# Attention with beacon tokens into a max-out FFN: quads' second halves by another queue, and a new opening order

## The chip, the cores and the metric

The kernel runs on one NeuronCore of a Trainium2 chip. The core has five instruction streams, each of which runs its own list in order: TensorE (PE, matrix products and transposes through it), VectorE (DVE), ScalarE (ACT), GpSimd (POOL) and SyncE (SP, which here only starts transfers). Transfers between the memory of the chip (HBM) and the core's on-chip memory are issued by SP, ACT or POOL, each to a queue of its own, and are carried out by 16 DMA engines. The metric is the time of one execution on the device in microseconds; of several executions the median is given.

## The reference

Eight batches of eight heads, 576 tokens of 64 features, and 16 "beacon" keys and values per head that every token may see. Causal attention over beacons and tokens is followed by an FFN that takes the maximum of three products:

```python
k_all = np.concatenate([beacon_k, k], axis=2)
v_all = np.concatenate([beacon_v, v], axis=2)
scores = scale * np.matmul(q, k_all.transpose(0, 1, 3, 2))
scores = np.where(causal, -1000000000.0, scores)
a = np.exp(scores - scores.max(-1, keepdims=True))
a /= a.sum(-1, keepdims=True) + 1e-09
attn = np.matmul(a, v_all)                      # (B, H, S, D)
x = attn.transpose(0, 2, 1, 3).reshape(4608, 512)
h = np.maximum(np.maximum(x @ w1, x @ w2), x @ w3)   # 512 -> 768
out = h @ w_out                                      # 768 -> 512
```

Inputs and output are FP32.

## The kernel before

All matrix work is done in BF16. Heads go in pairs (pair p is heads 2p and 2p+1 of its batch, with four pairs to a batch), and two pairs make a quad, that is half a batch. The order of every instruction is written out by hand: `first_steps` (line 901) is the opening and `loop_steps` (line 1075) is the rest. `emit_all` walks the lists, and each entry appends its instructions to the streams of the engines that it uses. An entry that stands early therefore also stands early on each of its engines, and an instruction that waits holds back everything behind it on that engine.

What the entries of the opening do:

- `load half p i` (`load_half`, line 221) brings the first 288 tokens of q (i = 0) or k (i = 1) of one pair as FP32 over the named queue, and `cast half` makes BF16 of it.
- `load quad half g h` (`load_quad`, line 237) brings half h of q and of k for the four heads of quad g of batch 0. It is issued by POOL, whose queue turns FP32 into BF16 on the way.
- `half p h bank q_copy idle idle_q` (`turn_half`, line 428) transposes q and k of one pair on PE (line 440) and copies the results into qT and kT (line 448): k by DVE, q by the named engine. `idle_q` and `idle` are numbers of pairs of filler transposes ahead of q's and of k's (`fill`, line 404).
- `load keys`, `cast keys`, `turn keys` bring the beacon keys, and `keys p` places a batch's beacon keys ahead of pair p's in kT.
- `scores p gi idle` (`emit_scores`, line 503) runs `idle` filler matmuls (`spare`, line 476), multiplies kT and qT for group gi of pair p (line 514) into one of two PSUM buffers, and ACT writes the exponential to `at_sb` (line 523). For batch 0, group 0 holds all that the first 288 tokens need.
- `mask p gi` (`emit_masks`, line 529) puts zeros above the diagonal, by DVE (line 540) or POOL (line 542).
- `load v0 t` and `cast v0 t` bring v of batch 0 in five tiles and cast them (line 328). A load with an engine's name is gated: that engine first writes one element of the destination, so the transfer is issued only when that engine has come so far in its list.
- `values quad hf` (`emit_pv`, line 561) sums the exponentials and multiplies them with v (line 583). `invert` (lines 604 and 606, ACT) and `multiply` (line 616, DVE) divide by the sums and write xT.
- `load w i` (`load_w`, line 335) brings one of the three FFN weights, as two transfers issued by POOL. `ffn bank kind` (`mm1_halves`, line 634) is one step of the FFN's first layer on 256 tokens: two column blocks, each over all four parts of the features, so it needs both transfers of its weight. DVE then copies the result (line 630) or takes the maximum with it (line 632).
- `load quad` and `whole` do for a quad of batch 1 what the halves do for batch 0; `load v`, `load pair` and `load` bring later batches by SP, in FP32, into eight staging buffers (`new_stage`, line 192) that are cast on chip.
- `busy n cols` is filler before any data has come.

After the opening four PSUM buffers are in use, and scores, FFN steps and the second layer alternate on PE to the end.

Of the kernel before, what the change touches and what calls it, by code (L numbers as in the profile page):

```python
# [9 lines left out]
BF16 = mybir.dt.bfloat16  # L10
# [6 lines left out]
def kernel(  # L17
# [15 lines left out]
    B, H, S, D = q.shape  # L33
# [12 lines left out]
    QP = S // QR  # L46
    HR = QR // 2
# [11 lines left out]
    PPQ = PPB // n_quad  # L59
# [41 lines left out]
    def head(g, j):  # L101
        return 4 * g + j
# [12 lines left out]
    early = early_stack.enter_context(tc.tile_pool(name="early", bufs=1))  # L115
# [42 lines left out]
    ring = [(sc_psum, "sc"), (sc_psum, "sc")]  # L158
# [30 lines left out]
    stage = {}  # L189
    v_tiles = {}  # L190

    def new_stage(key):
        stage[key] = st_pool.tile([128, STW], FP32, name="st")
        return stage[key]
# [21 lines left out]
    def half_source(g, h, i, j0, n):  # L216
        hs = slice(head(g, j0), head(g, j0) + n)
        src = (q, k)[i][0, hs, HALF * h : HALF * (h + 1)]
        return src.rearrange("h (p r) d -> p h (r d)", r=HR)

    def load_half(p, i, queue):
        st = half_pool.tile([QP, 2, HR, D], FP32, name=f"h32{i}")
        queue.dma_start(
            out=st.rearrange("p h r d -> p h (r d)"),
            in_=half_source(p // PPQ, 0, i, 2 * (p % PPQ), 2),
        )
        stage["half", p, i] = st
# [6 lines left out]
        )  # L234
        stage["half16", p, 0, i] = t16

    def load_quad(g, h):
        for i in range(2):
            t16 = early.tile([QP, 4, HR, D], BF16, name=f"quad{g}{h}{i}")
            nc.gpsimd.dma_start(  # L240
                out=t16.rearrange("p h r d -> p h (r d)"), in_=half_source(g, h, i, 0, 4)
            )
            for j in range(PPQ):
                stage["half16", PPQ * g + j, h, i] = t16[:, 2 * j : 2 * j + 2]

    def load_whole_quad(b, g):
        for i, src in enumerate((q, k)):
            t16 = early.tile([QP, 4, QR, D], BF16, name=f"whole{b}{g}{i}")
            nc.gpsimd.dma_start(
                out=t16.rearrange("p h r d -> p h (r d)"),  # L250
                in_=src[b, head(g, 0) : head(g, 4)].rearrange("h (p r) d -> p h (r d)", r=QR),
            )
            for j in range(PPQ):
                stage["whole", b * PPB + PPQ * g + j, i] = t16[:, 2 * j : 2 * j + 2]
# [94 lines left out]
    def load_beacons(b0, b1, dst, queue=None):  # L349
        for b in range(b0, b1):  # L350
            (queue or nc.sync).dma_start(
                out=dst[Nb * (b - b0) : Nb * (b - b0 + 1)],
                in_=beacon_k[b].rearrange("h n d -> n h d"),
            )
# [485 lines left out]
    def start_late():  # L840
# [9 lines left out]
    by = {"dve": by_dve, "act": by_act, "pool": by_pool}  # L850
    queue = {"sp": nc.sync, "act": nc.scalar, "q pool": nc.gpsimd}
    idle = {"dve": nc.vector, "pool": nc.gpsimd}
# [3 lines left out]
        "identity": lambda: make_identity(nc, ident),  # L856
        "triangle": make_tri,
        "load half": lambda p, i, e: load_half(p, i, queue[e]),
        "load quad half": load_quad,
        "load keys 0": lambda e: load_beacons(0, 1, bk32_0, queue[e]),  # L860
        "load keys 1": lambda: load_beacons(1, B_PE, bk32_1),
        "load v0": load_first_v,
# [36 lines left out]
        "cast keys 2": lambda e: by[e](bk16, bk32),  # L899
    }  # L900
    first_steps = [
        ("load half", 0, 0, "sp"),
        ("busy", 27, 200),
        ("identity",),
        ("busy", 16, 160),
        ("triangle",),
        ("load quad half", 1, 0),
        ("load half", 1, 0, "act"),
        ("load half", 0, 1, "act"),
        ("cast half", 0, 1, "dve"),  # L910
        ("load keys 0", "act"),
        ("cast keys 0", "act"),
        ("load half", 1, 1, "sp"),
        ("cast half", 0, 0, "act"),
        ("turn keys 0",),
        ("cast half", 1, 0, "pool"),
        ("load v0", 0, "pool"),
        ("cast half", 1, 1, "dve"),
        ("load v0", 1, "pool"),
        ("half", 0, 0, "ffn", "act", 0, 8),  # L920
        ("keys", 1, "act"),
        ("load v0", 2),
        ("half", 1, 0, "pv", "act", 3, 5),
        ("keys", 3, "pool"),
        ("load quad half", 0, 1),
        ("scores", 0, 0, 0),
        ("scores", 1, 0, 0),
        ("load w", 0),
        ("half", 3, 0, "ffn", "dve", 0, 0),
        ("half", 2, 0, "pv", "dve", 4, 0),  # L930
        ("mask", 1, 0, "dve"),
        ("cast v0", 0, "pool"),
        ("cast v0", 1, "act"),
        ("scores", 3, 0, 0),
        ("mask", 0, 0, "dve"),
        ("load v0", 3, "dve"),
        ("keys", 2, "pool"),
        ("cast v0", 2, "act"),
        ("scores", 2, 0, 7),
        ("values", 0, 0, "pv", 0, 4, 0),  # L940
        ("half", 0, 1, "ffn", "act", 0, 9),
        ("invert",),
        ("mask", 3, 0, "dve"),
        ("multiply",),
        ("scores", 0, 2, 4),
        ("mask", 2, 0, "pool"),
        ("load keys 1",),
        ("scores", 0, 3, 0),
        ("values", 1, 0, "ffn", 0, 4, 0),
        ("load quad half", 1, 1),  # L950
        ("invert",),
        ("multiply",),
        ("mask", 0, 2, "pool"),
        ("scores", 0, 1, 0),
        ("half", 1, 1, "pv", "act", 1, 0),
        ("load v0", 4, "dve"),
        ("scores", 1, 2, 4),
        ("mask", 0, 1, "pool"),
        ("cast v0", 3, "act"),
        ("ffn", "ring", 0),  # L960
        ("ffn", "ffn", 0),
        ("mask", 1, 2, "dve"),
        ("scores", 1, 3, 0),
        ("scores", 1, 1, 0),
        ("half", 2, 1, "pv", "dve", 0, 0),
        ("mask", 1, 3, "dve"),
        ("ffn", "ffn", 0),
        ("half", 3, 1, "pv", "dve", 0, 0),
        ("load v", 1, 0, "dve"),
        ("cast v0", 4, "dve"),  # L970
        ("mask", 0, 3, "dve"),
        ("mask", 1, 1, "dve"),
        ("scores", 2, 3, 0),
        ("scores", 2, 2, 7),
        ("load w", 1),
        ("scores", 3, 2, 0),
        ("mask", 2, 3, "dve"),
        ("cast keys 1", "dve"),
        ("values", 0, 1, "pv", 0, 4, 0),
        ("turn keys 1",),  # L980
        ("invert",),
        ("scores", 3, 3, 0),
        ("ffn", "ffn", 0),
        ("load quad", 1, 0),
        ("load w", 2),
        ("mask", 3, 3, "dve"),
        ("multiply",),
        ("load pair", 9, "pool"),
        ("scores", 2, 1, 0),
        ("mask", 2, 2, "pool"),  # L990
        ("ffn", "ffn", 0),
        ("mask", 2, 1, "pool"),
        ("scores", 3, 1, 0),
        ("keys", 6, "dve"),
        ("keys", 4, "pool"),
        ("ffn", "ring", 0),
        ("mask", 3, 1, "dve"),
        ("keys", 5, "dve"),
        ("mask", 3, 2, "pool"),
        ("whole", 4, "ffn", "dve"),  # L1000
        ("values", 1, 1, "pv+", 0, 4, 0),
        ("invert",),
        ("scores", 4, 1, 0),
        ("multiply",),
# [722 lines left out]
```

## Time and profile before

| what | value |
|---|---|
| median of 3 runs | 285.77 us (285.26 to 286.31) |
| the profiled execution | 285.21 us, span 283.3 us |
| PE busy | 276.3 us, 98% of the span |
| DVE, ACT, POOL busy | 176.5, 154.5, 143.4 us |
| the first scores on PE | at 8.75 us |
| the first FFN step on PE | at 19.47 us |

The span is the part of the execution in which the program's instructions run; the time contains some two microseconds around it. A row of the timeline or of the chain begins with the start and the length of a piece of work in us, then the engine, the name of what it writes and the line. A row of the waits names who waited for whom, for how long in total, how often, and the longest. A row of the groups ends with busy time, the mean in ns, and the idle time ahead of the group. A row on transfers gives their number, the size of one and the us from issue to landing. A row of the windows has the stretch, its length, each engine's busy time with its number of instructions, the granted share of PE's clock, and the busy time of the DMA engines as a share, which is over 1 where several queues are served at once.

### The profile page before, as it was taken

Reading aid. Unit: us, or ns where it says so; the run is one execution under the profiler, and the core shown is the slowest. Engines: PE = TensorE matmul, PEld = TensorE weight load, DVE = VectorE, ACT = ScalarE, POOL = GpSimd, SP = SyncE. Lnnn points to the kernel's source line nnn. Section 1 sums busy time; section 2 is a strip of 40 time slices with the busy share of each in tenths; the row PEclk is TensorE's granted clock in tenths of the full one; section 3 lists DMA queues with packets and bytes.
Section 4 is the critical chain, followed back from the end, with each engine's and each line's share of the span. In section 5 each row is a group of like instructions: output and inputs, shape, how many; then the busy total and the mean of one; then the engine's idle time right before and its main releaser. Section 6 shows DMA issues by size and latency. Waiting matters only on the chain.

```text
span 283.3 us, 11781 instructions
## 1 busy us (share of the span) xinstructions
PE 276.3 (98%) x5099; PEld 201.5 (71%) x5099; DVE 176.5 (62%) x331; ACT 154.5 (55%) x249; POOL 143.4 (51%) x316
## 2 busy tenths in 40 slices
PE   8999999999999999999999999999999999999995
PEld 7666777757777576768677686767877687757762
DVE  2456777886676765756566666646575665661754
ACT  2876676897563574637464574725765474624000
POOL 4462318898741583758734497508854682400000
PEclk9999999999999999999999999999999999999999
DMA  9999999999978399999999969989999962003004
GB/s 153 168 171 206 223 234 157 247 206 309 211 141 168 45 252 178 171 197 147 189 178 215 236 91 176 166 204 185 217 160 170 163 177 76 2 3 150 2 2 185
DMA packets 118307, 46.27 MB, mean 163 GB/s; under 512 B 107248, under 2 KB 112880, under 8 KB 118256
## 3 DMA queue, kind: packets, MB, share of 16 engines
q1 hardware_dynamic: 111888, 39.20, 75.6%
q0 software_dynamic: 5808, 6.00, 13.0%
q8 instruction: 40, 0.66, 1.1%
q10 hardware_dynamic: 560, 0.33, 0.4%
q14 instruction: 11, 0.09, 0.1%
HBM read 35.13 MB, written 9.44 MB: 157 GB/s over the span
## 4 chain that ended last, share of the span: by engine, by line
PE 91%; DMA 3%; ACT 2%; POOL 1%; DVE 1%; issue 1%; ACTq 0%; POOLq 0%
PE t L700 44%; PE t L726 16%; PE t L583 11%; PE t L514 6%; DMA quad<-in_k_dram 3%; PE pv L478 2%; ACT at_sb L523 2%; PE pv L638 2%; PE sc L514 1%; PE sc L638 1%; PE fps L638 1%; PE t L398 1%; POOL at_sb L542 1%; PE wide L583 1%; PE pv L583 1%
## 5 line engine op out<-in xcount | busy, mean ns | idle before, releaser
L700 PE MATMUL t<-xT,w_sb 64*128 64x288 bf16 (+1 forms) x1008 | 129.6, 285 | 0.0
L700 PE MATMUL t<-xC,wC 64*128 64x288 bf16 (+1 forms) x1008 | 129.6, 285 | 0.0
L523 ACT ACTIVATE at_sb<-t 128x992 bf16<-128x992 f32 (+1 forms) x96 | 82.6, 863 | 42.8 <-PE t L514 37.1
L632 DVE TENSOR_TENSOR hT<-hT,t 128x576 bf16<-128x576 bf16 (+1 forms) x84 | 63.7, 763 | 30.6 <-PE t L700 30.6
L542 POOL TENSOR_SCALAR_AFFINE_SELECT at_sb<-at_sb 128x256 bf16<-128x256 bf16 (+2 forms) x143 | 53.6, 390 | 53.7 <-ACT at_sb L523 41.2
L700 PEld LDWEIGHTS <-w_sb 64*128 64x128 bf16 x1008 | 51.3, 94 | 12.6 <-issue 1.1
L700 PEld LDWEIGHTS <-wC 64*128 64x128 bf16 x1008 | 51.0, 94 | 12.4
L726 PE MATMUL t<-w_out_sb,hT 128*128 128x512 bf16 x210 | 47.9, 380 | 0.0
L681 POOL COPY xC<-xT 64x576 bf16<-64x576 bf16 (+1 forms) x26 | 18.0, 693 | 42.8 <-DVE xT L616 42.5
L630 DVE CAST hT<-t 128x576 bf16<-128x576 f32 (+1 forms) x36 | 27.7, 769 | 14.8 <-PE t L700 14.6
L726 PEld LDWEIGHTS <-hT 128*128 128x128 bf16 x210 | 19.3, 98 | 22.8 <-issue 0.9
L259 POOL CAST p<-st 96x768 bf16<-96x768 f32 x44 | 34.9, 822 | 0.3
L734 DVE COPY y<-t 128x1024 f32<-128x1024 f32 (+1 forms) x20 | 21.8, 1091 | 20.5 <-PE t L726 20.3
L514 PE MATMUL t<-qT,kT 64*128 64x288 bf16 (+4 forms) x288 | 33.1, 279 | 0.0
L616 DVE TENSOR_TENSOR xT<-t,recip 128x288 bf16<-128x288 f32 (+2 forms) x78 | 22.9, 351 | 16.0 <-ACT recip L606 10.7
L604 ACT ACTIVATE lnd<-t 128x288 f32<-128x288 f32 x26 | 10.7, 410 | 36.9 <-PE t L583 36.9
L514 PEld LDWEIGHTS <-kT 64*128 64x128 bf16 x400 | 18.5, 94 | 11.4 <-issue 6.7
L583 PEld LDWEIGHTS <-v_sb 128*32 128x32 bf16 (+1 forms) x1408 | 24.6, 96 | 1.6 <-issue 0.4
L523 ACT ACTIVATE at_sb<-sc 128x736 bf16<-128x736 f32 (+5 forms) x28 | 23.2, 862 | 4.2 <-PE sc L514 4.1
L583 PE MATMUL t<-at_sb,v_sb 128*32 128x96 bf16 (+8 forms) x1144 | 23.3, 228 | 0.0
L316 POOL CAST v_sb<-st 128x1536 bf16<-128x1536 f32 (+2 forms) x21 | 18.4, 894 | 0.6 <-DMA st<-in_v_dram 0.6
L583 PEld LDWEIGHTS <-ones 128*32 128x32 bf16 (+2 forms) x512 | 10.9, 95 | 6.7 <-issue 3.9
(125 smaller groups left out, 220.1 us busy)
## 6 DMA issues: line engine op xcount, KB each, us to landing
out_dram<-y SPq DMA_DIRECT2D x15, 512.0 KB, 4.6
st<-in_q_dram SPq DMA_DIRECT2D x24, 288.0 KB, 5.8
st<-in_k_dram SPq DMA_DIRECT2D x24, 288.0 KB, 6.2
st<-in_v_dram SPq DMA_DIRECT2D x24, 256.0 KB, 5.5
w_sb<-in_moe_w_dram POOLq DMA_DIRECT2D x6, 384.0 KB, 8.9
st<-in_v_dram SPq DMA_DIRECT2D x8, 224.0 KB, 5.1
st<-in_v_dram SPq DMA_DIRECT2D x8, 160.0 KB, 4.7
out_dram<-y SPq DMA_DIRECT2D x5, 256.0 KB, 4.6
```

The costliest lines, as they stand in the source:

```text
L259: cast(t16.rearrange("p r h d -> p h r d"), st[0:QP, i * NQ2 : (i + 1) * NQ2].rearrange("p (h r d) -> p h r d", h=2, r=QR),)
L316: cast(v_sb[0:n, t:t1].rearrange("p t h d -> p (t h d)"), st[0:n, (t - t_lo) * H * D : (t1 - t_lo) * H * D],)
L514: nc.tensor.matmul(ps[:, e, off : off + q1 - q0], kT[hs, 128 * t : 128 * t + 128], qT[hs, q0:q1], start=True, stop=True, tile_position=(64 ...
L523: nc.scalar.activation(out=both_heads(p, gi), in_=ps[:, :, 0 : g_width(p, gi)], func=AF.Exp, scale=scale)
L542: nc.gpsimd.affine_select(out=view, in_=view, compare_op=ALU.is_ge, fill=0.0, base=x0, pattern=[[0, 2], [1, hi - lo]], channel_multiplier=-1,)
L583: nc.tensor.matmul(ps[bank][32 * j : 32 * j + 32, lo + q0 - qa : lo + qb - qa], lhsT, at_view(PPQ * quad + j // 2, t, j % 2, q0, qb), star ...
L616: nc.vector.tensor_mul(xT[:, 2 * g + part - 1, c0 + ca : c0 + cb], ps[bank][:, lo : lo + cb - ca], recip[:, ca:cb],)
L630: (by_i or by_dve)(h, ps)
L632: nc.vector.tensor_max(h, h, ps)
L700: nc.tensor.matmul(ps[:, e], w[own(e), ct, cols], x, start=(ct == 0 and not over), stop=(ct == n_ct - 1 and over), tile_position=(64 * e, 0),)
L726: nc.tensor.matmul(ps[:, u], h_tile(tt + u, ft), w_out_sb[:, ft, :], start=(ft == 0), stop=(ft == n_ft - 1),)
L734: nc.vector.tensor_copy(y[:, 0:n], ps[:, 0:n])
```

## The change

The two second halves of batch 0's quads are issued by SP instead of POOL. They land as FP32, q and k of a quad side by side in one of the eight staging buffers, and a new step casts each of them into the tile in which it landed before. Quad 1's is gated by POOL. The opening's list is put in another order, from the first load to the load of the third weight: other queues carry the first halves, pair 1's scores go first and pair 0's after `half 3 0` and `half 2 0`, the tiles of v come in the order 0, 2, 1, several casts and masks go to other engines, the first weight is loaded behind pair 1's mask, and the numbers of fillers differ. `load pair 9` stands eleven entries further down.

```diff
-    def load_quad(g, h):
+    def load_quad(g, h, queue=None, gate=None):
+        if queue:
+            st = new_stage(("quad", g, h))[0:QP].rearrange("p (i x) -> p i x", i=2)
+            if gate:
+                gate.memset(st[0:1, 0, 0:1], 0.0)
+            for i in range(2):
+                queue.dma_start(
+                    out=st[:, i].rearrange("p (h x) -> p h x", h=4),
+                    in_=half_source(g, h, i, 0, 4),
+                )
+            return
...
+    def cast_quad(g, h, i, cast):
+        st = stage["quad", g, h][0:QP].rearrange("p (i x) -> p i x", i=2)
+        t16 = early.tile([QP, 4, HR, D], BF16, name=f"quad{g}{h}{i}")
+        cast(t16.rearrange("p h r d -> p (h r d)"), st[:, i])
+        for j in range(PPQ):
+            stage["half16", PPQ * g + j, h, i] = t16[:, 2 * j : 2 * j + 2]
+        if ("half16", PPQ * g, h, 1 - i) in stage:
+            stage.pop(("quad", g, h))
...
 first_steps = [
-    ("load half", 0, 0, "sp"),
+    ("load half", 0, 0, "act"),
+    ("load quad half", 1, 0),
     ("busy", 27, 200),
     ("identity",),
     ("busy", 16, 160),
-    ("triangle",),
-    ("load quad half", 1, 0),
-    ("load half", 1, 0, "act"),
     ("load half", 0, 1, "act"),
-    ("cast half", 0, 1, "dve"),
+    ("load half", 1, 1, "act"),
     ("load keys 0", "act"),
+    ("cast half", 0, 0, "dve"),
+    ("load half", 1, 0, "sp"),
+    ("cast half", 0, 1, "act"),
     ("cast keys 0", "act"),
-    ("load half", 1, 1, "sp"),
-    ("cast half", 0, 0, "act"),
+    ("load v0", 0, "dve"),
+    ("half", 0, 0, "pv", "dve", 6, 0),
     ("turn keys 0",),
     ("cast half", 1, 0, "pool"),
-    ("load v0", 0, "pool"),
     ("cast half", 1, 1, "dve"),
+    ("load v0", 2, "pool"),
     ("load v0", 1, "pool"),
-    ("half", 0, 0, "ffn", "act", 0, 8),
+    ("keys", 3, "pool"),
+    ("half", 1, 0, "pv", "act", 0, 0),
     ("keys", 1, "act"),
-    ("load v0", 2),
-    ("half", 1, 0, "pv", "act", 3, 5),
-    ("keys", 3, "pool"),
-    ("load quad half", 0, 1),
-    ("scores", 0, 0, 0),
-    ("scores", 1, 0, 0),
+    ("triangle",),
+    ("scores", 1, 0, 4),
+    ("keys", 2, "pool"),
+    ("cast v0", 0, "dve"),
+    ("mask", 1, 0, "pool"),
+    ("load quad half", 0, 1, "sp"),
+    ("load v0", 3, "dve"),
     ("load w", 0),
     ("half", 3, 0, "ffn", "dve", 0, 0),
-    ("half", 2, 0, "pv", "dve", 4, 0),
-    ("mask", 1, 0, "dve"),
-    ("cast v0", 0, "pool"),
     ("cast v0", 1, "act"),
+    ("half", 2, 0, "pv", "dve", 6, 8),
+    ("scores", 0, 0, 0),
+    ("mask", 0, 0, "dve"),
     ("scores", 3, 0, 0),
-    ("mask", 0, 0, "dve"),
-    ("load v0", 3, "dve"),
-    ("keys", 2, "pool"),
+    ("cast quad half", 0, 1, 0, "dve"),
     ("cast v0", 2, "act"),
-    ("scores", 2, 0, 7),
+    ("scores", 2, 0, 0),
     ("values", 0, 0, "pv", 0, 4, 0),
-    ("half", 0, 1, "ffn", "act", 0, 9),
-    ("invert",),
-    ("mask", 3, 0, "dve"),
+    ("mask", 2, 0, "dve"),
+    ("cast quad half", 0, 1, 1, "pool"),
+    ("load keys 1",),
+    ("half", 0, 1, "ffn", "act", 8, 0),
+    ("invert",),
     ("multiply",),
-    ("scores", 0, 2, 4),
-    ("mask", 2, 0, "pool"),
-    ("load keys 1",),
+    ("scores", 0, 2, 3),
+    ("mask", 3, 0, "pool"),
+    ("load quad half", 1, 1, "sp", "pool"),
     ("scores", 0, 3, 0),
     ("values", 1, 0, "ffn", 0, 4, 0),
-    ("load quad half", 1, 1),
-    ("invert",),
+    ("invert",),
+    ("mask", 0, 2, "pool"),
+    ("load w", 1),
+    ("cast v0", 3, "dve"),
+    ("half", 1, 1, "pv", "act", 1, 0),
     ("multiply",),
-    ("mask", 0, 2, "pool"),
     ("scores", 0, 1, 0),
-    ("half", 1, 1, "pv", "act", 1, 0),
-    ("load v0", 4, "dve"),
-    ("scores", 1, 2, 4),
-    ("mask", 0, 1, "pool"),
-    ("cast v0", 3, "act"),
-    ("ffn", "ring", 0),
+    ("scores", 1, 2, 5),
+    ("load v0", 4),
     ("ffn", "ffn", 0),
-    ("mask", 1, 2, "dve"),
     ("scores", 1, 3, 0),
     ("scores", 1, 1, 0),
+    ("cast quad half", 1, 1, 1, "pool"),
+    ("mask", 0, 1, "pool"),
+    ("cast quad half", 1, 1, 0, "dve"),
+    ("ffn", "ffn", 0),
     ("half", 2, 1, "pv", "dve", 0, 0),
+    ("ffn", "ring", 0),
+    ("half", 3, 1, "pv", "act", 0, 6),
+    ("load quad", 1, 0),
+    ("mask", 1, 1, "pool"),
+    ("scores", 2, 3, 0),
     ("mask", 1, 3, "dve"),
-    ("ffn", "ffn", 0),
-    ("half", 3, 1, "pv", "dve", 0, 0),
-    ("load v", 1, 0, "dve"),
-    ("cast v0", 4, "dve"),
-    ("mask", 0, 3, "dve"),
-    ("mask", 1, 1, "dve"),
-    ("scores", 2, 3, 0),
-    ("scores", 2, 2, 7),
-    ("load w", 1),
+    ("cast keys 1", "dve"),
+    ("mask", 1, 2, "dve"),
+    ("mask", 0, 3, "pool"),
+    ("scores", 2, 2, 0),
     ("scores", 3, 2, 0),
     ("mask", 2, 3, "dve"),
-    ("cast keys 1", "dve"),
+    ("cast v0", 4, "dve"),
     ("values", 0, 1, "pv", 0, 4, 0),
+    ("invert",),
     ("turn keys 1",),
-    ("invert",),
     ("scores", 3, 3, 0),
     ("ffn", "ffn", 0),
-    ("load quad", 1, 0),
     ("load w", 2),
+    ("load v", 1, 0, "dve"),
+    ("multiply",),
     ("mask", 3, 3, "dve"),
-    ("multiply",),
-    ("load pair", 9, "pool"),
     ("scores", 2, 1, 0),
-    ("mask", 2, 2, "pool"),
     ("ffn", "ffn", 0),
     ("mask", 2, 1, "pool"),
     ("scores", 3, 1, 0),
-    ("keys", 6, "dve"),
     ("keys", 4, "pool"),
+    ("mask", 2, 2, "pool"),
     ("ffn", "ring", 0),
     ("mask", 3, 1, "dve"),
+    ("keys", 6, "dve"),
     ("keys", 5, "dve"),
     ("mask", 3, 2, "pool"),
     ("whole", 4, "ffn", "dve"),
     ("values", 1, 1, "pv+", 0, 4, 0),
+    ("load pair", 9, "pool"),
     ("invert",),
     ("scores", 4, 1, 0),
     ("multiply",),
```

More of the change, by code (lines that the diff above doesn't have):

```diff
@@ L858 @@
         "load half": lambda p, i, e: load_half(p, i, queue[e]),
-        "load quad half": load_quad,
+        "load quad half": lambda g, h, e=None, gate=None: load_quad(
+            g, h, e and queue[e], gate and idle[gate]
+        ),
+        "cast quad half": lambda g, h, i, e: cast_quad(g, h, i, by[e]),
         "load keys 0": lambda e: load_beacons(0, 1, bk32_0, queue[e]),
```

## The prediction

> **What bounds the kernel now.** I read the page's busy times first, then the waits of TensorE (PE), then busy time by stretch, then the chain that ended last.
>
> ```profile
> span 283.3 us, 11781 instructions
> ...
> PE 276.3 (98%) x5099; PEld 201.5 (71%) x5099; DVE 176.5 (62%) x331; ACT 154.5 (55%) x249; POOL 143.4 (51%) x316
> ```
>
> ```profile
> PE sc L514 <- DVE kT L448: 0.7, 2, 0.5
> PE pv L440 <- DMA quad<-in_k_dram: 0.6, 1, 0.6
> PE sc L514 <- ACT qT L448: 0.6, 1, 0.6
> PE sc L514 <- DVE qT L453: 0.4, 1, 0.4
> ```
>
> ```profile
> core 0: us, PE busy (x) PEld busy (x) DVE busy (x) ACT busy (x) POOL busy (x), PEclk, DMA share, GB/s
> 7.20:14.10 6.90, 6.19 (x169) 4.49 (x171) 3.52 (x13) 6.03 (x12) 3.42 (x8) 1.00 1.22 167
> ...
> 60.00:283.30 223.30, 220.08 (x4001) 160.20 (x3999) 137.65 (x220) 112.77 (x181) 111.86 (x244) 1.00 0.84 155
> ```
>
> PE is the bound: 276.3 of 283.3 us. Apart from its first start, every wait of PE that the waits list is in the opening. All but the last (0.4, at about 34 us, which comes of `whole 4` and which the change leaves) lie between 9 and 23 us: 0.7 + 0.6 + 0.6 = 1.9 us. The clock granted to PE is 1.00. From 60 us on PE is 220.08 of 223.30 us busy in steps that the change does not touch. So the change is worth what it does to the time at which PE has finished the opening's work, and two things can change there: waits, and filler (matmuls on the constant tile `busy`, whose results nobody reads).
>
> ```profile
> L478 PE MATMUL sc<-busy 128*128 128x320 bf16 x22 | 3.7, 301 | 0.0
> ...
> L408 PEld LDWEIGHTS <-busy 96*64 96x64 bf16 x60 | 1.7, 110 | 0.1
> ```
>
> The chain that ended last gives what they take of PE, and shows what the opening runs on:
>
> ```profile
> 7.38 0.46 PE fps L408 x16
> 7.84 0.25 PE fps L440 x12
> ...
> 9.18 1.43 ACT at_sb L523 x2
> ...
> 11.01 0.62 ACT v_sb L328
> 11.63 0.92 ACT at_sb L523
> 12.55 0.51 ACT v_sb L328
> 13.06 0.93 ACT at_sb L523
> ...
> 14.06 0.95 POOL at_sb L542 x3
> ...
> 15.65 7.10 DMA quad<-in_k_dram
> ...
> 24.69 1.06 PE sc L478 x7
> ...
> 26.17 1.65 PE pv L583 x68
> ```
>
> A filler matmul is 1.06/7 = 0.151 us, a filler transpose 0.46/16 = 0.029, a real transpose 0.25/12 = 0.021. The 22 and 60 fillers are 3.3 + 1.7 = 5.0 us; with the 1.9 us of waits, 6.9 us is all that a better order could ever gain. In the chain ScalarE (ACT) runs four exponentials and two casts of v without a break from 9.18 to 13.99. The last exponential releases a mask on POOL, behind which POOL issues the loads of the second quad's second half; its k lands 7.10 us later and PE waits for it.
>
> **The change, part by part.**
>
> *Filler.* The new order asks for 4 + 3 + 5 = 12 filler matmuls and 2 x (6 + 6 + 8 + 8 + 1 + 6) = 70 filler transposes: -10 x 0.151 + 10 x 0.029 = -1.22 us. This is a gain only where no wait takes its place.
>
> *The start.* Durations and hand-over times:
>
> ```profile
> 8.75 0.40 PE L514 MATMUL sc<-qT,kT 64*128 64x288 bf16 x6
> ...
> 11.00 0.40 PE L514 MATMUL sc<-qT,kT 64*128 64x288 bf16 x6 [0.46 <-DVE kT L448]
> ...
> 19.47 1.20 PE L638 MATMUL sc<-xT,w_sb 128*128 128x256 bf16 x8
> ```
>
> ```profile
> 5.70 0.63 DVE L231 CAST h<-h 96x384 bf16<-96x384 f32 x2 [3.89 <-DMA h<-in_k_dram]
> ...
> 10.40 0.45 DVE L448 COPY kT<-fps 128x288 bf16<-128x288 bf16 x1
> ...
> 16.01 0.89 DVE L616 TENSOR_TENSOR xT<-pv,recip 128x288 bf16<-128x288 f32 x3
> ```
>
> ```profile
> bk<-in_beacon_k_dram ACTq DMA_DIRECT2D x1, 32.0 KB, 4.4
> ```
>
> A copy that ends at 10.85 on VectorE (DVE) lets PE start at 11.00: 0.15 us. Batch 0's beacon keys are now the fourth load of ACT's queue, not the third: issued some 0.5 us later and landed, at 4.4 us, near 7.0 instead of 6.2. That is covered, since `half 0 0` goes ahead of `turn keys 0` and holds PE until about 7.75 (0.25 of transposes and 0.35 of filler from 7.13). What is not covered is the cast of pair 1's k half: it stands in DVE's queue behind both copies of `half 0 0`. These end at about 8.4, the cast (0.35) at 8.7, PE can turn that half at 8.85, DVE copies it by 9.65, and the first scores, pair 1's, start at 9.8 where they start at 8.75 now. So the exponentials begin 1.05 later. From there ACT works through exponential 1, a cast of v, exponentials 0 and 3, a cast, exponential 2 at the chain's 0.92 and 0.51, with a hole of 0.3 while PE does `half 3 0` and `half 2 0` (0.5 of transposes, 28 x 0.029 = 0.8 of filler) ahead of pair 0's scores: the last ends at 15.3 instead of 14.0. PE waits about 0.6 for a score buffer and 0.4 in the first `values`, which now waits for the second cast of v (14.4).
>
> *The quads.* Quad 0's second halves leave POOL for SP, right behind three v tiles. They come as FP32 and are cast by DVE (about 0.7, twice the 0.35 for half the columns) and POOL:
>
> ```profile
> L259 POOL CAST p<-st 96x768 bf16<-96x768 f32 x44 | 34.9, 822 | 0.3
> ```
>
> Both casts lie ahead of `half 0 1`, which PE reaches at 15.1: nothing. Quad 1's are gated by a memset on POOL behind pair 3's mask, at about 15.0, hence hardly earlier than the 15.65 of the chain. How long SP's queue takes with a weight moving beside it is not shown for this form. The nearest rows are 4.4 (above, no weight beside it) and this one, issued while the first weight moved:
>
> ```profile
> bk<-in_beacon_k_dram SPq DMA_DIRECT2D x1, 32.0 KB, 8.4
> ```
>
> It lands at 19.5 to 23.9. I take 21, a little under the chain's 22.75, as it is not queued behind the weight on its own queue. With 0.82 of casting it is ready by 22, and `half 2 1` comes at 22.9. So the 0.6 us wait of today goes, and the cast is hidden. At 23.9 it would cost 1.8.
>
> *The first weight.* `load w 0` is moved past `triangle`, `keys 2` and pair 1's mask on POOL. That mask waits for the first exponential (11.3) and takes the chain's 0.95. So the issue goes from 9.65 to about 12.3:
>
> ```profile
> 9.65 1.11 POOL L338 DMA_DIRECT2D w_sb<-in_moe_w_dram x2
> ```
>
> ```profile
> w_sb<-in_moe_w_dram POOLq DMA_DIRECT2D x1, 384.0 KB, 9.6
> ```
>
> ```profile
> w_sb<-in_moe_w_dram POOLq DMA_DIRECT2D x1, 384.0 KB, 8.2
> ```
>
> These are the second halves of the first and the second weight, the first with a quad ahead on the same queue, the second with little. The second half, issued at 12.85, lands at 21.05 or 22.45. PE wants it 0.26 us into the first FFN step. That step starts when xT is whole: `values` of quad 1 ends at 18.4, logarithm and exponential follow,
>
> ```profile
> 17.09 0.41 ACT L604 ACTIVATE lnd<-fps 128x288 f32<-128x288 f32 x1
> 17.54 0.44 ACT L606 ACTIVATE recip<-lnd 128x288 f32<-128x288 f32 x1
> ```
>
> and 0.89 of multiplies: 20.3 (today's first step: 19.47). The wait is 0.4 or 1.8; I take 0.4, as the quads have left this queue.
>
> [...]
>
> *The rest of the list.* The second weight is issued behind pair 0's mask at about 18, over 1 us earlier; the whole quad of batch 1 at about 21, the third weight at 24, two later, needed only after 37: nothing. `load v 1 0` has its gate on DVE behind the fourth FFN step, some 3.5 us later. Its cover is thin: POOL waits for that v already.
>
> ```profile
> L316 POOL CAST v_sb<-st 128x1536 bf16<-128x1536 f32 (+2 forms) x21 | 18.4, 894 | 0.6 <-DMA st<-in_v_dram 0.6
> ```
>
> The cost lies between 0 and 3.5; I take 0, the value nearest to today's landing, since the two weights and the quad that move beside that v are issued, taken together, no later than now. Two more staging buffers are in use, all free again by 23 us.
>
> *The sum.* From the first FFN step PE has three of them (2.95), two scores (0.45), two halves (0.5) and 0.35 of filler: 20.3 + 4.25 = 24.55, where today the same work is done at 24.4. Today 0.23 of scores, 1.06 of filler and 0.42 of scores lead to the last `values` of quad 0 at 26.17. In the new order there is no filler, but DVE is the later one:
>
> ```profile
> 23.53 0.23 DVE L540 TENSOR_TENSOR at_sb<-at_sb,tri 128x160 bf16<-128x160 bf16 x1
> 24.13 0.69 DVE L630 CAST hT<-fps 128x512 bf16<-128x512 f32 x1 [0.37 <-PE fps L638]
> ...
> 26.54 0.41 DVE L878 CAST bk<-bk 48x512 bf16<-48x512 f32 x1
> ```
>
> The second FFN step's copy ends at 23.7 (0.69), then come two copies of `half 2 1` (24.45), the third FFN step's copy (25.1), k of `half 3 1` (25.5), and a mask, a cast of keys and the mask that `values` needs (0.23, 0.41, 0.23 with some overlap): 26.1. So the last `values` of quad 0 starts at 26.1 without the weight's wait: a saving of 0.1, nearly all of the filler and of the quad's wait having been spent on the later start. With the wait of 0.4: +0.3 us. The profiled execution took 285.21, so 285.5 against it; it stands 0.56 below the median of 285.77, and against that the forecast is 286.1.
>
> **The rivals.**
>
> *Faster: the late start is made up.* If the exponentials start no later than 9.3 (k of pair 1 cast before the copies need DVE), or if what is lost is again slack that PE had filled, both savings stand: -1.22 - 0.56 = -1.8, or 284.0. For it: filler is where PE would have idled. Against it: DVE's fixed order at 8.4. It decides if the first FFN step starts by 18.8.
>
> *Slower: the first weight.* The second half lands at 22.45, PE waits 1.8, the sum is +1.7: 287.5. For it: today that half lands at 19.8, when the first FFN step begins, and it is issued 2.65 us later. Against it: no quad stands ahead of it on its queue any more. It decides once the half lands after 21.5.
>
> *Slower: the move does not do what it says.* Quad 1's halves land at 23.9 by the 8.4 row, are cast by 24.7, and PE waits 1.8 in place of 0.6: again 287.5, or more with the weight's wait on top. Against it: the 4.4 row.
>
> *Slower: v of batch 1* lands late, POOL's masks with it: up to +3.5, 289. I give it little.
>
> **How the numbers follow.** 0.5% is 1.4 us, about what a measurement of this kernel can tell from no change. My forecast, 286.1 with its own range of 285.0 to 287.0, has a chance of 0.5 and counts as the same. The faster rival has 0.2; the weight 0.17, the quad 0.09, v 0.04, together 0.3 slower. The range from 284.0 to 288.0 takes in the faster rival and the first two slower ones.
>
> **What would show it.** Right: the first exponential at about 10.2 and not 9.2; no wait of PE for a quad; the first FFN step between 20 and 21 us with a short wait for the first weight; the last `values` of quad 0 within 0.5 us of 26.2; PE as dense as before from 35 us on. Wrong: a first exponential before 9.5, or a first FFN step before 19 (then faster); a wait of PE for the weight or DVE's cast of over 1 us (then slower); any new wait behind 35 us.

## The result: slower, and a clock that fell

The changed kernel takes 289.38 us (median; 287.5 to 291.19) where the kernel before takes 285.37 (median of six): a ratio of 1.0138, 95% interval 1.0093 to 1.0183. Executions more than 1.5% above the fastest of their kernel are left out of the medians and ratios below: two of six with the transport alone, and one of twelve in each of two other runs. The forecast was 286.1 with a range up to 288.0, so the time lies outside it, on the slower side. The page of the changed kernel:

```profile
span 287.9 us, 11765 instructions
...
PE 277.7 (96%) x5085; PEld 201.3 (70%) x5099; DVE 178.4 (62%) x330; ACT 154.5 (54%) x248; POOL 143.7 (50%) x319
...
PEclk9957999999999999999999999999999999999999
```

The last line gives PE's granted clock in 40 slices of 7.2 us, in tenths. Before, every digit was a 9. Here the third and fourth are 5 and 7. The windows view (columns as in the prediction) puts edges on it:

```profile
core 0: us, PE busy (x) PEld busy (x) DVE busy (x) ACT busy (x) POOL busy (x), PEclk, DMA share, GB/s
...
11.30:14.70 3.40, 1.58 (x42) 1.17 (x36) 1.59 (x7) 2.45 (x4) 2.05 (x6) 1.00 1.23 232
14.70:24.90 10.20, 10.20 (x152) 5.49 (x149) 3.91 (x13) 6.80 (x13) 5.23 (x11) 0.50 1.06 206
```

From 14.7 to 24.9 us PE ran at half its clock. The clock fell in the other executions too: over the six, its mean lies between 0.980 and 0.994. PE looks busier than ever in that stretch (10.20 of 10.20 us), because each instruction takes longer: the 32 matmuls with v of one `values` take 1.40 us there (at 19.76) where they take 0.97 before (at 16.29); 152 matmuls fit into the stretch. In the 3.4 us ahead of it PE was busy for 1.58 us only. The waits of PE and its timeline show why:

```profile
PE sc L533 <- ACT at_sb L542: 2.3, 2, 1.8
PE sc L379 <- ACT bk L886: 1.4, 1, 1.4
```

```profile
8.72 0.25 PE L379 MATMUL sc<-ident,bk 16*128 16x16 bf16 x4 [1.42 <-ACT bk L886]
...
9.99 0.40 PE L533 MATMUL sc<-qT,kT 64*128 64x288 bf16 x6
...
13.99 0.40 PE L533 MATMUL sc<-qT,kT 64*128 64x288 bf16 x6 [1.82 <-ACT at_sb L542]
...
24.19 1.42 PE L657 MATMUL fps<-xT,w_sb 128*128 128x256 bf16 x8
```

(Lines are 19 higher than before from `turn_half` on: L533 is the scores, L542 the exponential, L602 `values`, L657 the FFN step.) There are two holes: 1.42 us at 7.30, for the beacon keys, and 1.82 at 12.17, for a score buffer. The first scores are 1.24 later than before (9.99 against 8.75), and the first FFN step 4.7 later (24.19 against 19.47). The chain that ended last gives the cause of the second hole:

```profile
6.05 6.27 DMA st<-in_v_dram
...
12.40 0.62 ACT v_sb L347
13.02 0.93 ACT at_sb L542
...
13.99 0.40 PE sc L533 x6
...
30.32 1.61 PE pv L602 x75
```

The second tile of v, now issued third, lands 6.27 us after its issue. ACT stands waiting to cast it, pair 0's exponential stands behind that cast, and PE, about to compute pair 2's scores, waits for the buffer which that exponential reads. The last `values` of quad 0 (the last line) starts at 30.32, where the prediction's fence has 26.17: 4.15 us later. The span ends 4.6 later. So the loss is made in the opening, some three quarters of it between 10 and 24 us. What remains to settle is how much of it is the clock, how much the order, and how much the quads' new way.

### The profile page after: what moved, and what is told of

It reads as the page before. It is cut to its first block, busy times and chain, and to the rows that moved or that the text cites. A ratio compares the mean times of both kernels' runs of the same rounds, so it can differ in the third digit from the quotient of the medians.

```text
span 287.9 us, 11765 instructions
## 1 busy us (share of the span) xinstructions
PE 277.7 (96%) x5085; PEld 201.3 (70%) x5099; DVE 178.4 (62%) x330; ACT 154.5 (54%) x248; POOL 143.7 (50%) x319
## 4 chain that ended last, share of the span: by engine, by line
PE 91%; DMA 3%; ACT 2%; issue 1%; POOL 1%; SPq 0%; DVE 0%; POOLq 0%; ACTq 0%
PE t L719 44%; PE t L745 16%; PE t L602 10%; PE t L533 6%; DMA st<-in_v_dram 2%; PE pv L657 2%; PE sc L533 2%; PE pv L602 2%; PE sc L657 2%; PE fps L657 2%; ACT at_sb L542 1%; DMA h<-in_q_dram 1%; PE sc L497 1%; PE t L417 1%; PE fps L602 1%
## 5 line engine op out<-in xcount | busy, mean ns | idle before, releaser
L542 ACT ACTIVATE at_sb<-t 128x992 bf16<-128x992 f32 (+1 forms) x96 | 82.6, 863 | 42.7 <-PE t L533 37.5
L561 POOL TENSOR_SCALAR_AFFINE_SELECT at_sb<-at_sb 128x256 bf16<-128x256 bf16 (+3 forms) x148 | 55.2, 389 | 53.6 <-ACT at_sb L542 42.6
L745 PE MATMUL t<-w_out_sb,hT 128*128 128x512 bf16 x196 | 47.2, 380 | 0.7
L533 PE MATMUL t<-qT,kT 64*128 64x288 bf16 (+4 forms) x288 | 33.0, 279 | 0.0
L635 DVE TENSOR_TENSOR xT<-t,recip 128x288 bf16<-128x288 f32 (+2 forms) x78 | 23.0, 351 | 15.8 <-ACT recip L625 11.5
L533 PEld LDWEIGHTS <-kT 64*128 64x128 bf16 x400 | 18.3, 95 | 12.7 <-issue 7.2
L542 ACT ACTIVATE at_sb<-sc 128x736 bf16<-128x736 f32 (+5 forms) x28 | 23.2, 862 | 6.0 <-PE sc L533 6.0
L602 PEld LDWEIGHTS <-v_sb 128*32 128x32 bf16 (+1 forms) x1408 | 24.8, 97 | 2.3 <-issue 0.4
L602 PE MATMUL t<-at_sb,v_sb 128*32 128x96 bf16 (+8 forms) x1144 | 23.3, 228 | 0.0
L657 PEld LDWEIGHTS <-w_sb 128*128 128x128 bf16 x144 | 13.2, 99 | 4.2 <-issue 2.2
## 6 DMA issues: line engine op xcount, KB each, us to landing
st<-in_q_dram SPq DMA_DIRECT2D x26, 288.0 KB, 5.4
st<-in_k_dram SPq DMA_DIRECT2D x26, 288.0 KB, 6.1
```

What stands on the lines that cost most here:

```text
L533: nc.tensor.matmul(ps[:, e, off : off + q1 - q0], kT[hs, 128 * t : 128 * t + 128], qT[hs, q0:q1], start=True, stop=True, tile_position=(64 ...
L542: nc.scalar.activation(out=both_heads(p, gi), in_=ps[:, :, 0 : g_width(p, gi)], func=AF.Exp, scale=scale)
L561: nc.gpsimd.affine_select(out=view, in_=view, compare_op=ALU.is_ge, fill=0.0, base=x0, pattern=[[0, 2], [1, hi - lo]], channel_multiplier=-1,)
L602: nc.tensor.matmul(ps[bank][32 * j : 32 * j + 32, lo + q0 - qa : lo + qb - qa], lhsT, at_view(PPQ * quad + j // 2, t, j % 2, q0, qb), star ...
L635: nc.vector.tensor_mul(xT[:, 2 * g + part - 1, c0 + ca : c0 + cb], ps[bank][:, lo : lo + cb - ca], recip[:, ca:cb],)
L657: nc.tensor.matmul(ps[:, f], w_in[i][:, ct, 128 * (ft + f) : 128 * (ft + f + 1)], xT[:, ct, lo : lo + MID], start=(ct == 0), stop=(ct == n ...
```

## The experiments

Theory A: the holes make the clock fall, and the half clock is most of the loss. Theory B: the chain of exponentials and casts simply runs later, and the clock is of little account. A third, C, lays the loss on the transport by SP. Each run below has a ratio to the kernel before, from runs on the same chip.

**Filler in the two holes.** `fill n` runs n filler matmuls into a fresh score buffer. The second filler stands ahead of pair 3's scores, one step before the hole, which is ahead of pair 2's.

```diff
+        ("fill", 9),
         ("turn keys 0",),
...
-        ("scores", 3, 0, 0),
+        ("scores", 3, 0, 10),
```

> The changed kernel with filler matmuls in its two holes on PE, nothing else: 9 ahead of turning the beacon keys (hole of 1.4 us at 7.3) and 10 ahead of pair 3's scores (hole of 1.8 us at 12.2). Theory A, the clock: the holes made the granted clock fall to 0.50 from 14.7 to 24.9 us, and the half clock costs PE most of the loss. Then the clock stays 1.00 to the end of the opening, the first FFN step starts near 21.5 instead of 24.2, and the time falls by 2 to 3 us to about 286.5. Theory B, the later start alone: the exponentials and casts that PE waits for set the time, clock or not. Then the clock may stay up, but the time stays within 0.5 us of 289.

287.93 us, ratio 1.0100 (1.0077 to 1.0123): 1.45 below the changed kernel by medians, less than the 2 to 3 expected, and the two intervals overlap. The effect on the opening is plain. The clock stays up in all six executions (0.998 to 1.000), and in the profiled ones the first FFN step comes at 20.63, not 24.19:

```profile
14.70:24.90 10.20, 9.05 (x179) 5.71 (x172) 6.13 (x18) 8.09 (x14) 4.82 (x11) 1.00 1.09 206
```

```profile
20.63 1.05 PE L657 MATMUL fps<-xT,w_sb 128*128 128x256 bf16 x8
...
24.15 0.32 PE L459 MATMUL pv<-ident,quad 96*64 96x96 bf16 x6 [0.81 <-POOL quad L259]
```

The same FFN step takes 1.05 us instead of 1.42. Of the 3.56 us that the step gains, part is given back: PE, now early, waits 0.81 us for POOL's cast of quad 1's k. At about 54 us, where the opening's effect has settled, this execution is still 2.9 us ahead of the changed kernel's (the table in the account below), as theory A expected; over 1 us of it is lost later, and the waits there explain only some of that. Theory B's "within 0.5 us of 289" falls.

**No filler in the kernel before.** All 82 fillers behind the warm-up are taken out; nothing else is touched.

```diff
-        ("half", 0, 0, "ffn", "act", 0, 8),
+        ("half", 0, 0, "ffn", "act", 0, 0),
...
-        ("scores", 2, 0, 7),
+        ("scores", 2, 0, 0),
```

> The kernel before without the 82 fillers behind the first warm-up (all counts in its halves and scores set to 0), nothing else. It tests the prediction's claim that filler only fills waits. Theory A (clock): the waits stand open then, up to 1 us each, the granted clock falls to 0.50 for 10 us of the opening, and the time rises by 2 to 4 us to 287.5 to 289.5. Theory B (filler is dead weight or cover, and the clock is of no account): the time stays within 0.7 us of 285.4, or falls a little.

290.42 us, ratio 1.0188 (1.0144 to 1.0232). Removing work made the kernel 4.7 us slower. Its windows:

```profile
8.10:11.50 3.40, 1.93 (x46) 1.45 (x48) 2.56 (x10) 3.04 (x6) 3.21 (x6) 1.00 1.37 188
11.50:25.20 13.70, 12.69 (x169) 7.22 (x166) 5.85 (x22) 9.23 (x16) 6.62 (x14) 0.50 1.04 175
```

No single hole between 5 and 11.5 us is over 0.63 us, yet over 3.4 us PE was busy for 1.93 only, and then had half its clock for 13.7 us. The mean clock of all six executions is 0.971 to 0.982. This is the plainest evidence that the filler does more than fill: its 5.0 us of PE time, which the prediction counted as what a better order could gain, hold the clock up. The 4.7 us are not all the price of this fall, though. The profiled execution is the slowest of the six (293.21 us), and at 54 us it trails the kernel before by only 1.7 (54.63 against 52.96, see the account below); it loses the rest later, partly in PE stops of up to 2.5 us (last section), the longest of which is followed by half the clock for another 3.4 us, from 62.7.

**v's tiles in order.**

```diff
-        ("load v0", 2, "pool"),
         ("load v0", 1, "pool"),
+        ("load v0", 2, "pool"),
```

> The changed kernel with v's second tile issued ahead of its third again (order 0, 1, 2), nothing else. ACT's cast of the second tile should then wait until about 11 and not 12.3, pair 0's exponential start at about 11.9 instead of 12.9, and the hole on PE shrink from 1.8 us to 0.8. Theory A (clock): the hole was long enough only through that wait, so the clock stays up and the time falls by 3 us or more, to 286 or less. Theory B (later start): the time falls by the 1.0 us of the wait, to about 288.

289.23 us, ratio 1.0132 (1.0105 to 1.0159): nothing gained. The hole did shrink, from 1.82 to 0.89 us, but the clock fell all the same, one microsecond later:

```profile
12.40:15.80 3.40, 2.40 (x65) 1.53 (x64) 1.89 (x7) 3.30 (x7) 2.48 (x6) 0.99 1.25 213
15.80:26.00 10.20, 10.18 (x109) 5.03 (x110) 3.85 (x12) 5.17 (x9) 3.96 (x9) 0.50 1.07 206
```

Neither theory's time came. This cause of the second hole was real, but mending it alone did not suffice. What is left of the hole ends at 12.64, and of the 1.00 us in which PE stood idle in the first of these rows 0.64 are another stop, between two fillers:

```profile
15.82 0.53 PE L427 MATMUL fps<-ident,busy 96*64 96x96 bf16 x7 [0.64 <-issue]
```

Of the six executions one kept its clock (mean 1.000) and still took 288.4 us, 0.8 less than the median: in that execution most of the loss is not the clock's.

**The beacon keys third in ACT's queue.**

```diff
+        ("load keys 0", "act"),
         ("load half", 1, 1, "act"),
-        ("load keys 0", "act"),
```

> The changed kernel with the beacon keys third in ACT's queue again, ahead of k of pair 1, nothing else. The keys should land near 7.4 instead of 8.0 and k of pair 1 near 8.0, so the first hole on PE shrinks from 1.4 to about 0.8 us, and the first scores start at about 9.7 instead of 10.0. Theory A (clock): the second hole stays, so the clock still halves, and the time changes by 0.5 us at most, unless the two holes together made it fall, in which case 286. Theory B (later start): 0.3 to 0.6 us less.

288.4 us, ratio 1.0106 (1.0072 to 1.0140). The first hole is gone but for 0.33 us, and the first scores start at 8.96, a full 1.03 us sooner where 0.3 was expected, but the second hole grows to 2.23 us, and the clock fell in the profiled execution. Here single executions say what the half clock costs. Over the six, three had a mean clock of 0.994 and took 287.14, 287.39 and 287.44 us, and three had 0.981 to 0.982 and took 289.36, 289.51 and 289.92. The difference in clock is 0.0125 of 288 us, that is 3.6 us less of full clock; in time it is 2.1 us between the medians.

**The transport alone**, at the old places in the old order, with the casts by DVE.

```diff
-        ("load quad half", 0, 1),
+        ("load quad half", 0, 1, "sp"),
...
         ("mask", 0, 0, "dve"),
+        ("cast quad half", 0, 1, 0, "dve"),
+        ("cast quad half", 0, 1, 1, "dve"),
...
-        ("load quad half", 1, 1),
+        ("load quad half", 1, 1, "sp", "pool"),
...
         ("mask", 1, 2, "dve"),
+        ("cast quad half", 1, 1, 0, "dve"),
+        ("cast quad half", 1, 1, 1, "dve"),
```

> The kernel before with one part of the change alone: the second halves of the quads issued by SP as FP32, at the old places in the list and with the old fillers, and cast by DVE. Theory A and theory B both put the loss in the new order, so they expect a time within 1 us of before (285 to 286.5), with a clock of 1.00. A third theory, C: the transport costs it (SP's queue is slower, v and quads delay each other, the casts load DVE). Then most of the loss, 3 us or more, stands here too, and PE waits for the quads.

290.54 us, ratio 1.0181 (1.0147 to 1.0214): C was right for this order, A and B wrong, as far as the profiled execution shows. In it (289.45 us) the clock stayed up (0.998 over the span), and PE waited instead:

```profile
PE pv L602 <- DVE at_sb L559: 1.8, 1, 1.8
...
PE pv L459 <- DVE quad L259: 1.0, 1, 1.0
```

```profile
st<-in_v_dram SPq DMA_DIRECT2D x1, 160.0 KB, 8.6
```

The last tile of v, issued at 20.11 us, lands 8.6 us later, where before it took 5.5. DVE waits for it with two masks behind the cast, which `values` needs: 1.8 us. The casts cost another 1.0 of waiting for quad 1. Together that is 2.8 us, and at 54 us this execution trails the kernel before by 2.9 (55.86 against 52.96). In the other three the clock was 0.994, 0.992 and 0.981, so there part of the loss is the clock's again. The old list had no room for the casts and the late tile.

**Three mends at once**: keys third, v in order, and filler for what is left of the holes (2 and 6).

```diff
+        ("load keys 0", "act"),
         ("load half", 1, 1, "act"),
-        ("load keys 0", "act"),
...
+        ("fill", 2),
         ("turn keys 0",),
...
-        ("load v0", 2, "pool"),
         ("load v0", 1, "pool"),
+        ("load v0", 2, "pool"),
...
-        ("scores", 3, 0, 0),
+        ("scores", 3, 0, 6),
```

> The changed kernel with three mends at once: the beacon keys third in ACT's queue, v's tiles in the order 0, 1, 2, and filler in what is left of the two holes (2 and 6 matmuls). Theory A with the later start as the rest of the loss: the clock stays 1.00, the first scores start at 9.0, the exponentials run on from there without a hole, and the time is 1 to 1.5 us below the run with filler alone, 286.4 to 287. If the quads' transport holds the rest, PE still waits 0.8 us or more for quad 1's k, and the time stays above 287.3.

287.17 us, ratio 1.0060 (1.0034 to 1.0086). The first scores are at 9.1 and the clock is up (one of the eleven executions fell, to 0.982 and 290.01 us), but PE waits for POOL's casts of both quads, 1.2 us in all, more for quad 0 than for quad 1, and later 0.3 for a pair that POOL casts, as in the changed kernel too:

```profile
PE fps L459 <- POOL quad L259: 0.9, 1, 0.9
...
PE pv L459 <- POOL quad L259: 0.4, 1, 0.4
PE pv L417 <- POOL p L278: 0.3, 1, 0.3
```

**The old transport in the new order**, with filler as in the first run.

```diff
         ("keys", 3, "pool"),
+        ("load quad half", 0, 1),
...
-        ("load quad half", 0, 1, "sp"),
...
-        ("cast quad half", 0, 1, 0, "dve"),
...
-        ("cast quad half", 0, 1, 1, "pool"),
...
-        ("load quad half", 1, 1, "sp", "pool"),
+        ("load quad half", 1, 1),
...
-        ("cast quad half", 1, 1, 1, "pool"),
...
-        ("cast quad half", 1, 1, 0, "dve"),
```

> The changed kernel's order with filler in both holes (as in the run with filler alone, 287.93), but with the quads' second halves by POOL's queue again, as BF16 and without casts: quad 0's behind the keys of pair 3, quad 1's behind pair 3's mask. If the transport costs what is left: the 0.8 us wait for quad 1's k goes and the time falls by 0.8 us or more, to 287.1 or less. If the order costs it: 287.5 to 288.5, since the first FFN step still starts at 20.6.

287.43 us, ratio 1.0056 (1.0031 to 1.0080): 0.5 below the run with filler alone, with overlapping intervals. The wait for quad 1 is gone; waits of 0.6 for a cast of v and 0.6 for the first weight stand in its place. The latter is the prediction's weight rival in small, since the quad is ahead of the weight on one queue again and the weight is issued late.

**The new order with the old transport, mended.** The three mends, and the quads by POOL's queue again, without casts: quad 0's and the first weight behind the keys of pair 3, their old place in that queue, and quad 1's behind pair 3's mask.

```diff
         ("keys", 3, "pool"),
+        ("load quad half", 0, 1),
+        ("load w", 0),
...
-        ("load quad half", 0, 1, "sp"),
...
-        ("load w", 0),
...
-        ("load quad half", 1, 1, "sp", "pool"),
+        ("load quad half", 1, 1),
...
```

> The run with three mends, with the quads and the first weight back on POOL's queue at the old place (behind the keys of pair 3), without casts: the new order without the new transport. If the transport holds the 1.5 us that the three mends leave, this is within 0.5 us of before, 285.3 to 286.2. If the order of scores and casts holds it, the time stays at 287.

285.52 us, ratio 1.0008 (0.9981 to 1.0035): the kernel before again. Against the three mends alone, it takes 1.65 us less, the two intervals only touching. So the new order of scores, casts and masks costs nothing that can be told once its holes are closed. With the holes closed, what is left is the transport, together with the weight's late issue, which this run undoes too.

**Earlier quad by SP, earlier weight by POOL.** The three mends, quad 1's half without its gate, the weight ahead of the mask.

```diff
+        ("load quad half", 1, 1, "sp"),
...
-        ("load quad half", 1, 1, "sp", "pool"),
...
         ("keys", 3, "pool"),
+        ("load w", 0),
...
-        ("load w", 0),
```

> As the run with three mends, with two more: quad 1's second half is issued by SP right behind quad 0's, without its gate, and the first weight by POOL behind the keys of pair 3, ahead of pair 1's mask. If quad 1's late landing (23.0 us) holds PE in the run with filler, its wait goes and the time falls by 0.8 us against the run with three mends, to about 285.7; if SP's queue merely delays what stands behind it (v's last two tiles, the keys of batches 1 to 3), a wait for one of these takes its place and nothing is gained.

291.51 us, ratio 1.0210 (1.0176 to 1.0245): 4.3 worse than the three mends, so a clear miss. PE's waits for the quads are gone, as hoped, but the clock fell in all six executions (0.981 to 0.988), in the profiled one at 16.7 us. Ahead of that PE stood still between two fillers of one and the same run:

```profile
17.84 0.85 PE L427 MATMUL fps<-ident,busy 96*64 96x96 bf16 x15 [2.14 <-issue]
```

Neither instruction needs data. What PE waited for the waits do not show (last section).

**The quad sooner in the kernel before.** One entry moved, so that POOL issues quad 1's second half while it would wait for an exponential.

```diff
+        ("load quad half", 1, 1),
         ("multiply",),
...
-        ("load quad half", 1, 1),
```

> The kernel before with one entry moved: POOL issues quad 1's second half as before, but ahead of pair 2's mask, for which it waits from 11.5 to 14.06 us, so some 3 us sooner. It lands by 20.5 instead of 22.75 and PE's wait of 0.56 us for it goes, with no new transport and no cast. If that wait is worth what it lasts, the time falls by 0.3 to 0.6 us; if it only lets another wait end later, it stays within 0.3 us; if the quad delays the first weight and the tiles of v, it rises.

285.16 us, ratio 0.9987 (0.9967 to 1.0007): no difference that can be told. The rows on transfers say why: q and k from issue to landing, before and then in this run:

```profile
quad<-in_q_dram POOLq DMA_DIRECT2D x1, 144.0 KB, 6.2
quad<-in_k_dram POOLq DMA_DIRECT2D x1, 144.0 KB, 7.1
```

```profile
quad<-in_q_dram POOLq DMA_DIRECT2D x1, 144.0 KB, 9.7
quad<-in_k_dram POOLq DMA_DIRECT2D x1, 144.0 KB, 10.4
```

Issued at 11.96 and 12.63 instead of 14.96 and 15.65, the halves land at 21.7 and 23.0 instead of 21.2 and 22.7. In the changed kernel SP issues k at 17.16 and it lands 5.9 later, at 23.0 too:

```profile
st<-in_q_dram SPq DMA_DIRECT2D x1, 288.0 KB, 5.1
st<-in_k_dram SPq DMA_DIRECT2D x1, 288.0 KB, 5.9
```

Three issues of k, spread over 4.5 us and two queues, lead to one landing time within 0.3 us. Within these 4.5 us, the wait that the prediction's chain showed behind the quad was thus not one for its issue or its queue. Issued sooner still, a half does land sooner, at the cost of what is behind it: with the earlier quad above, SP issued q at 9.48 and it landed at 17.17, but the tile of v behind it landed at 22.72, where the changed kernel has 16.54. What is left as the cause, by the author's estimate, is the traffic of the 16 DMA engines (their busy share from 14.7 to 24.9 us is 1.06 before and 1.06 in the changed kernel), the first weight's among it. No run tests this, nor whether it is this weight or the rest.

## Why the prediction was wrong

**The step that failed** is in its first part: "The clock granted to PE is 1.00" was read as a property of the kernel, and filler as matmuls that only take up time. In the sum this became -1.22 us of filler, with holes of 0.6 and 0.4 us in front of it as mere delay. The runs show the clock to be an outcome: of this very filler (taken out, the clock falls in all six executions and the time rises by 4.7 us, not all of it through the clock) and of the holes (filled, the clock stays at 1.00 and the first FFN step comes 3.56 us sooner). The prediction had no rival in which the clock falls.

What the traces show of these falls: they last 13.7, 10.2 and 3.4 us, that is four, three and one times 3.4 us. They do not follow the longest hole: one of 1.82, 0.89 or even 0.63 us went with a fall, while one of 1.8 us, with the transport alone, went with none. What went with the fall in these three runs is the busy time of PE over the 3.4 us ahead: 1.58 in the changed kernel, 1.93 without filler and 2.40 with v in order, of 3.40 us. In the kernel before it was 2.69 from 7.9 to 11.3 us and 2.75 from 9.0 to 12.4 us, and the clock stayed at 1.00.

**What was right.** Once the clock is held, the sum is nearly right as far as the first FFN step: it was put at 20.3 and comes at 20.63 in the run with filler. The weight was put at 21.05 and lands at 20.46 in the changed kernel and at 20.00 in the run with filler, and neither has a wait for it: the weight rival did not come.

**What came out by luck.** The first scores were put at 9.8 and came at 9.99, but not by the path of the prediction. It had pair 1's cast on DVE end at 8.7 and called the beacon keys, put at 7.0, covered. In the changed kernel that cast ends at 8.07, and PE waits 1.42 us for ACT's cast of the keys, which starts at 8.05:

```profile
7.72 0.35 DVE L231 CAST h<-h 96x384 bf16<-96x384 f32 x1
```

```profile
8.05 0.62 ACT L886 CAST bk<-bk 16x512 bf16<-16x512 f32 x1 [2.47 <-DMA bk<-in_beacon_k_dram]
```

With the keys third in their queue the first scores start at 8.96, so about 1 us of the late start is the keys'. Likewise, the rival of v of batch 1 was put at 289, next to the 289.38 that came, but POOL waits 0.0 us ahead of its casts of that v in the changed kernel: the number was met, the cause was not this.

**The mis-sized terms.** Behind the first exponential the prediction gave ACT a hole of 0.3 us, for PE's turning. It had no term for the new order of v's tiles: ACT waited 0.95 us for the second tile, now issued third, and PE's wait for the buffer was 1.82 in place of 0.6. Quad 1's k was put at 21, inside the 19.5 to 23.9 of its two rows; it landed at 23.0, close to the 22.75 of the kernel before. So the rival that the move does not do what it says, given 0.09, describes in part what happens once the clock is held: PE waits 0.81 us in the run with filler. The sum let the quads' wait of 0.6 go and the casts be hidden, and gave the weight's late issue 0.4; the three together cost about 1.6 us instead, by the two mended runs.

**The account.** The table gives each kernel's ratio, and the start of one logarithm of ACT's, the one that reads the tile `wide` (line 604 before, 623 after), in the profiled execution. It lies shortly after the opening and is the same piece of work in each kernel.

| kernel | ratio | the logarithm starts at, us |
|---|---|---|
| before | 1 | 52.96 |
| changed | 1.0138 | 57.33 |
| filler in the two holes | 1.0100 | 54.39 |
| three mends | 1.0060 | 54.02 |
| three mends, old transport and weight | 1.0008 | 52.86 |

In the opening, then, the changed kernel loses 4.4 us: 2.9 go when the holes are filled and the clock holds, 0.4 more when keys and v come in their old order, and 1.2 when transport and weight go back. These are single executions. By the ratios the three steps are worth about 1.1, 1.1 and 1.5 us of the whole time. Only the whole, the first step by its clock, and the last step by intervals that touch are well told apart; the middle one is not.

## What to carry to other kernels

Filler on PE need not be free time to be won back: here the kernel before took 4.7 us more without it. Before counting filler as a gain, add up PE's busy time over every 3.4 us of the new order. In these traces nine such stretches had PE at full clock and busy for 2.40 us or less; after six of them it had half its clock for 3.4 to 13.7 us, after three it had not. That is no sure rule, and no run shows whether it holds in another kernel. An issue a few us earlier or by another queue need not shorten the wait for a transfer: three issues of one transfer, 4.5 us apart at most, landed within 0.3 us of each other. Compare landing times, not issue times, and those of the transfers behind it too: the tile of v behind the earlier quad landed at 22.72 instead of 16.54 us. A cast that takes the place of a converting transfer needs its own gap in the list of the engine that does it: with the transport alone, PE waited 1.0 us for DVE's cast of quad 1.

## What the runs showed beside

Half the clock cost less here than it looks. At half clock for 10.2 us PE loses 5.1 us of full clock, but the executions of the run with the keys third, with the longer and the shorter fall, differ by 2.1 us for 3.4 to 3.6 us of clock. Presumably the rest falls into waits that were there anyway; no run separates it.

How little PE may be busy before its clock falls is open. In the twelve traces every change of the granted clock lies a whole number of 3.41 us behind its first rise (at 4.50 us in the changed kernel, where the step from one warm-up filler to the next falls from 0.167 to 0.086 us; the page has a 9 ahead of that too). Cut into such steps from that rise, and leaving out the last 8 us, the traces have nine in which PE had its full clock and was busy for 2.40 us or less. After six of them the clock fell (0.92 to 2.40 us busy), after three it did not (1.67 with the transport alone, 1.93 with the old transport, 2.29 without filler). So the place of the step does not explain the exceptions. Nor is it shown why a fall lasts one, three or four steps: in the changed kernel PE was busy throughout all three.

PE can also stop for something that the waits call "issue" and do not name. In the twelve traces there are nine such stops of over 0.5 us, the longest of 2.49 us in the run without filler. Each of them ends 1.35 to 1.63 us after a 16 KB transfer has ended on the DMA queue that the page lists as "q8 instruction". In the run with the earlier quad this transfer runs from 15.16 to 16.43 us, and PE goes on at 17.84. By the queue's name and this order in time the author's estimate is that PE was waiting for its own program; no run tests this. Such stops may be part of why single executions of the changed kernel scatter by 3.7 us, also at a like clock: 287.5 and 290.67 us, both at 0.994.
